# Accumulating block 1's first product pair by pair, with four accumulators in two PSUM banks

## The chip, the core and the metric

The kernel runs on one core of a Trainium2 chip. The metric is the device time of one execution in microseconds (us); of the kernel before, three timed runs gave 608.89, 608.99 and 609.29 us, median 608.99. Engines are called as the profile calls them: PE (TensorE), DVE (VectorE), ACT (ScalarE), POOL (GpSimd), and SP, whose queue issues all the loads spoken of here.

## The reference

A block-and-window attention over 2 batches, 8 heads, 768 positions and head size 64 is followed by two feed-forward layers on the 1536 resulting tokens of width 512:

```python
k_sum = k.reshape(B, H, nb, 32, D).max(axis=3)
v_sum = v.reshape(B, H, nb, 32, D).mean(axis=3)
scores = concat([where(abs(i - j) < 16, scale * q @ k.T, -1e9), scale * q @ k_sum.T + log(32)])
x = softmax(scores) @ concat([v, v_sum])          # tokens x 512
...
h = x @ w_in
x = (max(h, 0) + alpha * min(h, 0)) @ w_out       # 512 -> 2048 -> 512
...
h = x @ w_in
out = (h * sigmoid(h)) @ w_out                    # 512 -> 2048 -> 512
```

## The kernel before

Every fp32 product of the feed-forward layers is made of three fp32r matmuls on high and low pieces: `three` (lines 278 to 283) issues low weights by high input, high by low, and high by high into one PSUM tile. The attention works on blocks of `QB` = 256 tokens (six blocks) and on pairs of heads (four pairs), so it has 24 steps, numbered here 0 to 23 in the order of line 638: block 0 and block 1 alternate over the four pairs (steps 0 to 7), then blocks 2, 3, 4 and 5 follow with four steps each. A step runs through these stages:

- the scores `sc` on PE (L523), into the one PSUM tile that the pool `ps_s` has, so that the next step's scores wait until the last have been read;
- scale, mask and maximum, `t` (L531) and `nm` (L540), on DVE;
- the exponentials `e` with their sums `sm` on ACT (L548), the reciprocal `rs` on DVE (L557, L559), and the product of both on POOL (L560);
- the transposes `pt` on PE (L566), copied by ACT to `pT`; the values `o` on PE (L579), copied by ACT (`xh`, L587) and split by DVE (`xl`, L588).

Beside it run the preparations. `prep_k` makes block maxima of the keys on DVE (L465, L471); `prep_v1` sums the values on POOL (L482) and DVE (`vr`, L485). The weights are loaded by `load_next` (L116), turned from halves into high and low pieces by three DVE operations (L142, L146, L149), an ACT copy (L155) and a POOL subtraction (L156). The values of the second batch and the weights from the fourth tile on land in the same two buffers `raw` (pool `stage`, `STAGE` = 2), so a load waits until an earlier tile has been read.

The first feed-forward layer's first product of block 0 is made in `first_in` (line 719) one pair at a time, five steps behind the attention: four accumulators, each in a PSUM bank of its own, of which 256 of 512 columns are used. The pool `ps_mm` has six banks, and `pt`, `pv` and `o` rotate in what is left. Blocks 1 to 5 are made by `in_item` (line 296), which takes two of the four column tiles at once, all four pairs in a row, and so begins when the block's attention is done. `activate` makes both Relu halves on ACT (L324, L325), their sum on DVE (L328), a high piece on ACT (L336) and a low piece on POOL (L337); `out_pair` (line 345) makes the second product.

All this code is written out in the order of keys (`at`, line 644: a step's number plus the constants of lines 26 to 32). The tile framework then reorders it: it plays the instructions through on a timeline of its own and places each on its engine where it expects it to be ready. On the chip each engine keeps the order that results, so an instruction that waits holds all that is behind it on its engine.

The text counts *products*: the PE matmuls of L281 to L283, from the first on. Block 0's and block 1's first products are 48 each.

## Time and profile before

| | |
|---|---|
| median of three runs | 608.99 us (608.89 to 609.29) |
| span of the profiled execution, first to last instruction | 604.6 us |
| PE busy | 576.8 us, 95% of the span |
| DVE busy | 424.0 us, 70% |
| ACT busy | 277.5 us, 46% |
| POOL busy | 72.3 us, 12%, all of it in the first 160 us |

The profiled execution's time as a whole is not among the profile's figures; its span is 4.4 us under the median. Shares of the whole span hide the two parts of this kernel: PE is busy without a break after the first 64 us, while before that it has gaps and DVE has none. "Busy" counts the time from an instruction's start to its end, and a matmul's end is modelled: back to back, the next one starts well before the modelled end of the one before it.

### The profile page before, as it was taken

What the parts mean: (1) busy time and instruction counts of PE and PEld (TensorE: products, weight loads), DVE (VectorE), ACT (ScalarE), POOL (GpSimd) and SP (SyncE); (2) the same over time, 40 slices, a digit from 0 to 9 for tenths busy, and PEclk for the clock granted to TensorE, in tenths of its full rate; (3) what the DMA queues carried; (4) which work ended last, traced back from release to release, by engine and by line L of the source; (5) the groups of instructions that cost most, each with busy time, mean ns of one, the idle gap of its engine ahead of it and who ended that gap; (6) DMA issues with size and microseconds to landing.
All of it is one profiled execution on the core that took longest, in us unless ns stands there. A gap on an engine that the chain in (4) does not pass through costs nothing.

```text
span 604.6 us, 8927 instructions
## 1 busy us (share of the span) xinstructions
PE 576.8 (95%) x3428; PEld 483.5 (80%) x3428; DVE 424.0 (70%) x747; ACT 277.5 (46%) x636; POOL 72.3 (12%) x69
## 2 busy tenths in 40 slices
PE   2777999999999999999999999999999999999997
PEld 1556788999888888888888888888888888888886
DVE  3899979548995484349696879885972499965312
ACT  2768977654543341424544645543621245333200
POOL 2657654232100000000000000000000000000000
PEclk9988999999999999999999999999999999999999
DMA  9958754002351040003022002333130032200112
GB/s 263 341 193 260 231 147 140 2 2 70 140 154 56 0 140 0 1 1 112 28 69 70 1 1 79 131 117 93 32 108 0 1 111 96 73 1 0 54 69 88
DMA packets 31771, 52.54 MB, mean 87 GB/s; under 512 B 2288, under 2 KB 20976, under 8 KB 31728
## 3 DMA queue, kind: packets, MB, share of 16 engines
q1 hardware_dynamic: 31728, 51.97, 27.2%
q8 instruction: 27, 0.44, 0.3%
q14 instruction: 16, 0.13, 0.1%
HBM read 48.82 MB, written 3.15 MB: 86 GB/s over the span
## 4 chain that ended last, share of the span: by engine, by line
PE 82%; DVE 9%; DMA 3%; ACT 2%; SPq 1%; issue 1%; POOL 0%; DVEq 0%; POOLq 0%
PE ps L281 27%; PE ps L282 27%; PE ps L283 27%; DVE w L146 2%; DMA y<-in_w 1%; DVE w L149 1%; DMA vs<-in_vw 1%; DVE w L142 1%; DVE t L531 1%; DVE sm L557 1%; DVE nm L540 1%; PE o L579 1%; DVE kT L465 1%; ACT e L548 1%; DMA raw<-in_w 1%
## 5 line engine op out<-in xcount | busy, mean ns | idle before, releaser
L281 PE MATMUL ps<-xh,wl 128*128 128x512 f32 (+1 forms) x352 | 127.5, 367 | 1.2 <-ACT xh L587 1.2
L282 PE MATMUL ps<-xl,wh 128*128 128x512 f32 (+1 forms) x352 | 127.9, 364 | 0.0
L283 PE MATMUL ps<-xh,wh 128*128 128x512 f32 (+1 forms) x352 | 127.4, 363 | 0.0
L282 PE MATMUL ps<-gl,wh 128*128 128x512 f32 (+1 forms) x240 | 83.3, 348 | 0.0
L283 PE MATMUL ps<-gh,wh 128*128 128x512 f32 (+1 forms) x240 | 82.9, 346 | 0.0
L281 PE MATMUL ps<-gh,wl 128*128 128x512 f32 (+1 forms) x240 | 82.5, 350 | 0.0
L336 ACT CAST gh<-g 128x512 fp32r<-128x512 f32 x96 | 59.3, 622 | 46.2 <-PE ps L283 24.2
L281 PEld LDWEIGHTS ps<-xh,wl 128*128 128x128 f32 x352 | 66.5, 191 | 12.4 <-POOL e L560 1.4
L282 PEld LDWEIGHTS ps<-xl,wh 128*128 128x128 f32 x352 | 67.3, 191 | 10.2 <-issue 0.2
L283 PE MATMUL ps<-wh,gh 128*128 128x512 f32 (+1 forms) x196 | 75.4, 385 | 0.0
L283 PEld LDWEIGHTS ps<-xh,wh 128*128 128x128 f32 x352 | 67.3, 191 | 10.1
L282 PE MATMUL ps<-wl,gh 128*128 128x512 f32 (+1 forms) x196 | 75.4, 385 | 0.0
L281 PE MATMUL ps<-wh,gl 128*128 128x512 f32 (+1 forms) x196 | 75.2, 385 | 0.1
L337 DVE TENSOR_TENSOR gl<-g,gh 128x512 fp32r<-128x512 f32 x84 | 57.5, 687 | 20.7 <-ACT gh L336 20.3
L394 DVE TENSOR_TENSOR y<-ps,y 128x512 f32<-128x512 f32 x48 | 32.8, 689 | 45.4 <-PE ps L283 45.2
L324 ACT ACTIVATE g<-ps 128x512 f32<-128x512 f32 (+1 forms) x50 | 29.0, 579 | 70.8 <-PE ps L283 69.9
L155 ACT CAST wh<-w 128x512 fp32r<-128x512 f32 x64 | 39.3, 622 | 48.0 <-DVE w L149 43.5
L328 DVE SCALAR_TENSOR_TENSOR g<-m,nal,g 128x512 f32<-128x512 f32 (+1 forms) x60 | 41.4, 705 | 25.0 <-ACT m L325 24.9
L281 PEld LDWEIGHTS ps<-gh,wl 128*128 128x128 f32 x240 | 45.2, 189 | 6.6 <-issue 0.5
L282 PEld LDWEIGHTS ps<-gl,wh 128*128 128x128 f32 x240 | 45.4, 189 | 6.1 <-POOL gl L337 0.2
L283 PEld LDWEIGHTS ps<-gh,wh 128*128 128x128 f32 x240 | 45.3, 189 | 5.6
L146 DVE SCALAR_TENSOR_TENSOR w<-raw,w 128x512 uint32<-128x512 uint32 x61 | 44.6, 741 | 0.3
(82 smaller groups left out, 867.1 us busy)
## 6 DMA issues: line engine op xcount, KB each, us to landing
raw<-in_w SPq DMA_DIRECT2D x61, 512.0 KB, 3.8
vs<-in_vw SPq DMA_DIRECT2D x16, 288.0 KB, 5.6
kT<-in_kT SPq DMA_DIRECT2D x8, 480.0 KB, 5.2
q<-in_qT SPq DMA_DIRECT2D x24, 128.0 KB, 4.1
out<-y SPq DMA_DIRECT2D x11, 256.0 KB, 2.0
y<-in_vT SPq DMA_DIRECT2D x4, 384.0 KB, 6.5
y<-in_w SPq DMA_DIRECT2D x3, 512.0 KB, 7.7
raw<-in_vT SPq DMA_DIRECT2D x4, 384.0 KB, 4.5
```

The costliest lines, as they stand in the source:

```text
L142: nc.vector.tensor_scalar(out=w, in0=high, scalar1=3, scalar2=0x3FFFFFFF, op0=ALU.logical_shift_left, op1=ALU.bitwise_and,)
L146: nc.vector.scalar_tensor_tensor(out=w, in0=high, scalar=0xC0000000, in1=w, op0=ALU.bitwise_and, op1=ALU.bitwise_or)
L149: nc.vector.scalar_tensor_tensor(out=w, in0=low, scalar=29, in1=w, op0=ALU.logical_shift_right, op1=ALU.bitwise_or)
L155: nc.scalar.copy(out=hi, in_=w)
L281: nc.tensor.matmul(ps, all_, bh, start=first, stop=False)
L282: nc.tensor.matmul(ps, ah, bl, start=False, stop=False)
L283: nc.tensor.matmul(ps, ah, bh, start=False, stop=last)
L324: nc.scalar.activation(out=g[:, j * w:(j + 1) * w], in_=ps, func=AF.Relu)
L328: nc.vector.scalar_tensor_tensor(out=g[:, at], in0=m[:, at], scalar=nal[:, f + j:f + j + 1], in1=g[:, at], op0=ALU.mult, op1=ALU.add,)
L336: nc.scalar.copy(out=gh, in_=g)
L337: (nc.gpsimd if early else nc.vector).tensor_tensor(out=gl, in0=g, in1=gh, op=ALU.subtract)
L394: nc.vector.tensor_tensor(out=at, in0=src, in1=at, op=ALU.add)
```

## The change

`first_in` now takes the block as an argument and is called for blocks 0 and 1, each one pair at a time, again five steps behind. Block 1 is taken out of the list of `in_item`s, and the list that interleaves the two products is shifted, so that both items of a block's first product stand ahead of the second product of the block before. Two accumulators of 256 columns share one bank: the first one's first matmul clears the bank's flags, the second one's first matmul is issued without a clear, and a dependency without a semaphore keeps it behind the first. `activate` gets one bank of 512 columns in place of two of 256, so ACT reads it with two instructions in place of four. No matmul is added or taken away.

```diff
-    def three(ps, a, b, first, last):
+    def three(ps, a, b, first, last, again=False):
 
         (ah, all_), (bh, bl) = a, b
-        nc.tensor.matmul(ps, all_, bh, start=first, stop=False)
+        i = nc.tensor.matmul(ps, all_, bh, start=first, stop=False, skip_group_check=again)
...
+        return i
...
-    def in_k(u, i, k, ps):
+    def in_k(u, i, k, ps, first=None):
...
-            k == 0, k == KT - 1,
+            k == 0 if first is None else first, k == KT - 1, first is not None,
...
-        ins = [(i, in_item, units[i], f, 2) for i in range(1, NBLK) for f in range(0, CF, 2)]
+        ins = [(i, in_item, units[i], f, 2) for i in range(2, NBLK) for f in range(0, CF, 2)]
...
-            seq += ins[max(0, 2 * i - 1):2 * i + 1]
+            seq += ins[max(0, 2 * i - 2):2 * i] if i else []
...
-        def first_in(p):
-
-            if not acc:
-                acc.extend(ps_mm.tile([P, 512], F32, tag="mm", name="ps")[:, :QB] for _ in range(CF))
+        def first_in(blk, p):
+
+            if blk not in acc:
+                acc[blk] = [ps_mm.tile([P, 512], F32, tag="mm", name="ps") for _ in range(CF // 2)]
             need(p + 1)
-            for i in range(CF):
-                in_k(units[0], i, p, acc[i])
-                if p == NPAIR - 1 and i % 2:
-                    activate(units[0], i - 1, 2, acc[i - 1:i + 1])
+            for i in range(0, CF, 2):
+                ps = acc[blk][i // 2]
+                one = in_k(units[blk], i, p, ps[:, :QB], p == 0)
+                two = in_k(units[blk], i + 1, p, ps[:, QB:], False)
+                if p == 0:
+                    tc.add_manual_dep(
...
+                if p == NPAIR - 1:
+                    activate(units[blk], i, 2, [ps])
                     rests()
...
-            if blk == 0:
-                at(k + AT_IN, first_in, p)
+            if blk < 2:
+                at(k + AT_IN, first_in, blk, p)
```

The framework makes a new order of it on every engine. Two places are shown, as the built programs hold them (in the changed kernel lines after 283 are one higher).

The first is on DVE, around step 9's scores. Before, after `t` of step 9 come the last of the weight tile `w_305`, key maxima, and only much later the sum `vr` of the fifth tile of values, out of the buffer `raw_771`:

```order
L531 SCALAR_TENSOR_TENSOR t_642<-sc_633,cst_93 128x480
L146 SCALAR_TENSOR_TENSOR w_305<-raw_250,w_305 128x512
L465 TENSOR_REDUCE kT_599<-kT_599 128x24
L540 TENSOR_REDUCE nm_644<-t_642 128x4
L149 SCALAR_TENSOR_TENSOR w_305<-raw_250,w_305 128x512
L557 TENSOR_SCALAR sm_602<-sm_602 128x4
L588 TENSOR_TENSOR xl_79<-o_607,xh_78 128x256
L471 COPY kT_599<-kT_599 128x6x24
L531 SCALAR_TENSOR_TENSOR t_701<-sc_692,cst_93 128x480
L465 TENSOR_REDUCE kT_648<-kT_648 128x24
L559 RECIPROCAL rs_623<-sm_602 128x4
L485 TENSOR_REDUCE vr_965<-raw_771 128x24
```

After, that sum (here `vr_1020`, out of `raw_807`) stands ahead of step 9's `t`, and the next weight tile `w_1059` is begun ahead of step 10's `t`; it is loaded into the buffer that the sum has to free:

```order
L486 TENSOR_REDUCE vr_1020<-raw_807 128x24
L466 TENSOR_REDUCE kT_611<-kT_611 128x24
L532 SCALAR_TENSOR_TENSOR t_666<-sc_657,cst_93 128x480
L558 TENSOR_SCALAR sm_614<-sm_614 128x4
L472 COPY kT_611<-kT_611 128x6x24
L589 TENSOR_TENSOR xl_79<-o_619,xh_78 128x256
L541 TENSOR_REDUCE nm_668<-t_666 128x4
L560 RECIPROCAL rs_647<-sm_614 128x4
L142 TENSOR_SCALAR w_1059<-raw_1055 128x512
L532 SCALAR_TENSOR_TENSOR t_725<-sc_716,cst_93 128x480
```

So the sum has moved ahead of two steps' `t`, and the weight tile, which before began after step 12's `t`, ahead of step 10's.

The second place is where the scores of steps 17 to 20 stand. Before, DVE took step 17's `t` (`t_1331`) shortly after step 16's, ahead of the weight tile `w_1204`:

```order
L531 SCALAR_TENSOR_TENSOR t_1226<-sc_1217,cst_93 128x480
L485 TENSOR_REDUCE vr_1152<-raw_1063 128x24
L557 TENSOR_SCALAR sm_1130<-sm_1130 128x4
L540 TENSOR_REDUCE nm_1228<-t_1226 128x4
L559 RECIPROCAL rs_1162<-sm_1130 128x4
L588 TENSOR_TENSOR xl_79<-o_1044,xh_78 128x256
L531 SCALAR_TENSOR_TENSOR t_1331<-sc_1322,cst_93 128x480
L328 SCALAR_TENSOR_TENSOR g_873<-m_876,nal_77,g_873 128x256 x2
L142 TENSOR_SCALAR w_1204<-raw_1200 128x512
```

After, step 17's `t` (`t_1360`) stands behind four weight tiles, of which `w_2118` is the last, and behind the evacuation `y` of the second product's last tile of block 1:

```order
L142 TENSOR_SCALAR w_2118<-raw_1425 128x512
L589 TENSOR_TENSOR xl_79<-o_1293,xh_78 128x256
L146 SCALAR_TENSOR_TENSOR w_2118<-raw_1425,w_2118 128x512
L149 SCALAR_TENSOR_TENSOR w_2118<-raw_1425,w_2118 128x512
L359 COPY y_80<-ps_1325 128x2x256
L532 SCALAR_TENSOR_TENSOR t_1360<-sc_1351,cst_93 128x480
L329 SCALAR_TENSOR_TENSOR g_1219<-m_1222,nal_77,g_1219 128x256 x2
L589 TENSOR_TENSOR xl_79<-o_1382,xh_78 128x256
L142 TENSOR_SCALAR w_2154<-raw_1458 128x512
L541 TENSOR_REDUCE nm_1362<-t_1360 128x4
L532 SCALAR_TENSOR_TENSOR t_1419<-sc_1410,cst_93 128x480
```

On PE the scores of steps 18, 19 and 20 now stand close together, with nine products between the first two and one between the last two (`sc_1502` is step 19's, `sc_1578` step 20's, `ps_1460` block 3's first product; before, 38 products lie between steps 19 and 20):

```order
L281 MATMUL ps_1460<-xh_78,wl_159 128x256
L282 MATMUL ps_1460<-xl_79,wh_158 128x256
L283 MATMUL ps_1460<-xh_78,wh_158 128x256
L524 MATMUL sc_1502<-kT_855,q_1001 64x120 x8
L281 MATMUL ps_1460<-xh_78,wl_192 128x256
L524 MATMUL sc_1578<-kT_611,q_1065 64x120 x8
L282 MATMUL ps_1460<-xl_79,wh_191 128x256
L283 MATMUL ps_1460<-xh_78,wh_191 128x256
```

What moved: the score step whose reading on DVE was early now waits behind weight conversion, and three score steps follow each other with little other PE work between them.

## Rows read from the trace of the kernel before

**Rows 1.** Busy time by stretch: length, then PE, PEld, DVE, ACT, POOL, then clock, DMA.

```profile
36.00:64.00 28.00, 21.00 (x278) 16.92 (x279) 27.96 (x56) 22.82 (x83) 17.81 (x15) 0.88 0.70 212
64.00:102.00 38.00, 37.96 (x423) 33.66 (x422) 33.06 (x66) 30.96 (x94) 22.27 (x20) 1.00 0.60 174
```

**Rows 2.** Timeline of PE: start, length (us), line, tiles, count, idle time before.

```profile
77.86 0.65 PE L566 MATMUL pt<-cst,e 128*120 128x128 f32 x4
...
102.46 0.63 PE L523 MATMUL sc<-kT,q 64*64 64x120 f32 x14 [0.50 <-DVE t L531]
...
109.92 0.64 PE L523 MATMUL sc<-kT,q 64*64 64x120 f32 x16
```

**Rows 3.** Timeline of PE, two products in a row at full clock.

```profile
63.83 0.28 PE L283 MATMUL ps<-xh,wh 128*128 128x256 f32 x1
63.95 0.28 PE L281 MATMUL ps<-xh,wl 128*128 128x256 f32 x1
```

**Rows 4.** Timeline of DVE around steps 8 to 11.

```profile
45.74 0.91 DVE L149 SCALAR_TENSOR_TENSOR w<-raw,w 128x512 uint32<-128x512 uint32 x1
...
50.29 0.94 DVE L465 TENSOR_REDUCE kT<-kT 128x24 f32<-128x768 f32 x1
...
55.37 0.31 DVE L485 TENSOR_REDUCE vr<-raw 128x24 f32<-128x192 f32 x1
```

**Rows 5.** Timeline of SP's queue, two loads into the buffers `raw`.

```profile
46.67 0.33 SPq L450 DMA_DIRECT2D raw<-in_vT  x1
...
55.71 0.33 SPq L116 DMA_DIRECT2D raw<-in_w  x1
```

**Rows 6.** DMA issues from 46 to 47.2 us: count, size, us to landing.

```profile
raw<-in_vT SPq DMA_DIRECT2D x1, 384.0 KB, 4.2
```

**Rows 7.** Timeline of POOL, the sum of the fifth tile of values.

```profile
51.45 1.99 POOL L482 TENSOR_TENSOR raw<-raw 128x384 f32<-128x384 f32 x2
```

**Rows 8.** All loads into the buffers `raw` from 30 to 105 us.

```profile
DMA to landing us min/median/max: 3.3/3.8/5.6
```

**Rows 9.** Timeline of DVE in a stretch in which POOL stands idle.

```profile
98.57 0.68 DVE L358 COPY y<-ps 128x512 f32<-128x512 f32 x1
99.17 0.68 DVE L149 SCALAR_TENSOR_TENSOR w<-raw,w 128x512 uint32<-128x512 uint32 x1
99.77 0.42 DVE L142 TENSOR_SCALAR w<-raw 128x512 uint32<-128x512 uint32 x1
100.10 0.41 DVE L588 TENSOR_TENSOR xl<-o,xh 128x256 fp32r<-128x256 f32 x1
100.44 0.68 DVE L146 SCALAR_TENSOR_TENSOR w<-raw,w 128x512 uint32<-128x512 uint32 x1
101.15 0.69 DVE L149 SCALAR_TENSOR_TENSOR w<-raw,w 128x512 uint32<-128x512 uint32 x1
101.76 0.65 DVE L531 SCALAR_TENSOR_TENSOR t<-sc,cst 128x480 f32<-128x480 f32 x1
102.33 0.87 DVE L328 SCALAR_TENSOR_TENSOR g<-m,nal,g 128x256 f32<-128x256 f32 x2
103.11 0.64 DVE L540 TENSOR_REDUCE nm<-t 128x4 f32<-128x480 f32 x1
103.68 0.41 DVE L588 TENSOR_TENSOR xl<-o,xh 128x256 fp32r<-128x256 f32 x1
```

**Rows 10.** Timeline of DVE after step 16's scores.

```profile
74.47 0.63 DVE L531 SCALAR_TENSOR_TENSOR t<-sc,cst 128x480 f32<-128x480 f32 x1
75.02 0.34 DVE L485 TENSOR_REDUCE vr<-raw 128x24 f32<-128x192 f32 x1
...
79.78 0.43 DVE L142 TENSOR_SCALAR w<-raw 128x512 uint32<-128x512 uint32 x1
```

**Rows 11.** Timeline of all engines, one moment at which POOL and DVE both work.

```profile
34.22 1.01 POOL L560 TENSOR_TENSOR e<-e,rs 128x480 f32<-128x480 f32 x1 [0.85 <-DVE rs L559]
...
34.42 1.36 DVE L146 SCALAR_TENSOR_TENSOR w<-raw,w 128x512 uint32<-128x512 uint32 x1
```

More of the change, by code (lines that the diff above doesn't have):

```diff
@@ L276, in rests @@
             pending.pop(0)()
-    def three(ps, a, b, first, last):
+    def three(ps, a, b, first, last, again=False):
         (ah, all_), (bh, bl) = a, b
-        nc.tensor.matmul(ps, all_, bh, start=first, stop=False)
-        nc.tensor.matmul(ps, ah, bl, start=False, stop=False)
-        nc.tensor.matmul(ps, ah, bh, start=False, stop=last)
+        i = nc.tensor.matmul(ps, all_, bh, start=first, stop=False, skip_group_check=again)
+        nc.tensor.matmul(ps, ah, bl, start=False, stop=False, skip_group_check=again)
+        nc.tensor.matmul(ps, ah, bh, start=False, stop=last, skip_group_check=again)
+        return i
     g_t = {}
-    def in_k(u, i, k, ps):
+    def in_k(u, i, k, ps, first=None):
         l, ch, t0, n, _ = u
@@ L686, in tile_blocks_attention_mlps @@
         spread_t = {}
-        acc = []
+        acc = {}
         def means(b, p):
@@ L717, in need @@
                 conv_op(at_conv[0])
-        def first_in(p):
-            if not acc:
-                acc.extend(ps_mm.tile([P, 512], F32, tag="mm", name="ps")[:, :QB] for _ in range(CF))
+        def first_in(blk, p):
+            if blk not in acc:
+                acc[blk] = [ps_mm.tile([P, 512], F32, tag="mm", name="ps") for _ in range(CF // 2)]
             need(p + 1)
-            for i in range(CF):
-                in_k(units[0], i, p, acc[i])
-                if p == NPAIR - 1 and i % 2:
-                    activate(units[0], i - 1, 2, acc[i - 1:i + 1])
+            for i in range(0, CF, 2):
[4 more added lines that the diff above has]
+                    tc.add_manual_dep(
+                        two.ins if hasattr(two, "ins") else two,
+                        (one.ins if hasattr(one, "ins") else one).name,
+                        mybir.DependencyInfo(mybir.DependencyClass.NoSync, mybir.DependencyReason.DATA),
+                        reason="the bank is cleared by its first product",
+                    )
+                if p == NPAIR - 1:
+                    activate(units[blk], i, 2, [ps])
                     rests()
```

2 lines of the change are left out of this document (1 added, 1 removed).

## The prediction

> **What bounds the kernel now.** Read busy time by stretch first. From 64 us on PE never stops (37.96 of 38 us), so a microsecond by which PE gets ahead of its work before that point shortens the kernel by one, unless PE has to wait again later. From 36 to 64 us it is the other way round: DVE is busy 27.96 of 28 us and PE only 21.00 [rows 1]. PE's 7.0 idle us there are the room into which the change puts work; DVE, which sets when each step of the attention is done, has no room at all. Then read PE's timeline to see where the two meet again: the last time that PE waits for anything is 0.50 us at 102.46, for step 18's `t` on DVE [rows 2]. DVE is thus not far behind PE until 102 us, and an order that lets PE run ahead must let DVE run ahead too.
>
> One point serves to compare both kernels: the end of step 20's scores at 109.92 + 0.64 = 110.56 us [rows 2]. By the two orders exactly the same PE work stands ahead of it in both kernels once the later of step 18's transposes and step 20's scores is done (scores 0 to 20, transposes 0 to 18, values 0 to 16, 288 products). All that follows is the same work at full clock with no PE wait in the trace. So the new time is the old one plus the shift of this point. The median is 608.99 and the span 604.6; the 4.4 us around the span are taken as unchanged.
>
> **What the change moves.** Block 1's 48 products leave the stretch after step 13's scores and go between steps 6 and 15. One product costs 63.95 - 63.83 = 0.12 us at full clock [rows 3], so 48 x 0.12 = 5.8 us are moved, less than the 7.0 us of room. But PE's order ahead of step 16's scores shows 110 products in place of 84: only 26 net, 26 x 0.12 = 3.1 us, are gained there, since block 0's second product, which stood between, now stands behind. That is the most that PE can be ahead while DVE keeps its times. On ACT four reads of 256 columns become two of 512, counted as nothing, since ACT has 5.2 us of idle time in the stretch [rows 1]; the clear-free first matmul and the dependency without a semaphore stand on PE in order and cost nothing; the number of banks held for the accumulators is four as before, and that the last two are held some products longer is covered by the first two, which come free when block 0 ends.
>
> **What DVE pays.** Up to step 16's `t` DVE has the same instructions ahead of it in both orders, plus one `xl` (103.11 + 0.57 to 103.68 and 100.44 - 100.10 = 0.34 us [rows 9]). Two of them now come earlier than their data.
>
> First, the sum `vr` of the fifth tile of values. It stood at 55.37 us; in the new order it has the place, counted in DVE instructions, that the key maxima of 50.29 us have now [rows 4]. Its load may start when the weight tile before it in the buffer has been read, and that ended at 45.74 + 0.91 = 46.65 us, with the issue at 46.67 [rows 4, 5]; the new order reaches that point at about the same time or half a microsecond sooner. The load lands 4.2 us later [rows 6], POOL takes 1.99 us [rows 7]: 46.2 + 4.2 + 2.0 = 52.4. DVE gets there at 50.3 to 50.8, so it waits 1.6 to 2.1 us; I take 1.6. Second, the weight tile begun ahead of step 10's `t` is loaded into the buffer that this sum frees: 52.7 + 0.1 + 3.8 (median landing [rows 8]) = 56.6. Between the sum and the weight tile DVE has key maxima 0.9, `t` 0.57, `nm` 0.57, `xl` 0.34 and three small ones of 0.1 to 0.2, about 2.8 us, so it arrives at 55.5 and waits 1.1; with the wait of step 10's `t` behind it, PE, ACT and POOL can't go on with the attention. Together 2.7 us on an engine that had no idle time. Off go about 0.3 us for a wait that falls away and 0.3 us for DVE work that no longer runs against POOL. Step 16's `t` moves from 74.47 [rows 10] to 74.5 + 0.3 + 2.7 - 0.6 = 76.9, and step 16's scores, four short DVE instructions ahead of it, end at 76.4.
>
> PE has 110 products done then. Before, the 110th was done at 77.86 [rows 2], with step 17's scores (0.6) and one small transpose (0.2) done as well. So PE is ahead by 77.9 - 76.4 - 0.8 = 0.7 us at that point, not by 3.1.
>
> **What comes late next.** In the new order step 17's `t` stands behind four weight tiles on DVE, and a chain of buffers runs through them. 34 products take PE to 80.7; DVE evacuates the second product (0.6) and sums the last values (0.3) by 81.6; the next weight tile can be loaded only then. Before, that load was landed and begun at 79.78, 4.4 us after the end of the sum at 75.36 [rows 10]; by the median landing of 3.8 it is 85.5. The tile after that waits for the next sum (86.1 + 3.9 = 90.0), its three operations take 0.33 + 0.71 + 0.60 = 1.64 [rows 9], to 91.7, and free the buffer for the fourth one (95.6). The third tile, a `g` (0.78) and an evacuation (0.60), 3.0 us in all, fit in that gap. Then 0.33 + 0.34 + 0.71 + 0.60 + 0.60 bring step 17's `t` to 98.2, its end 98.7; `g`, `xl`, a weight operation and `nm` (0.78 + 0.34 + 0.33 + 0.57) bring step 18's `t` to 100.7 to 101.3; two weight operations, `nm` and a sum (0.71 + 0.60 + 0.57 + 0.1) bring step 19's to 103.3 to 103.9. PE can't cover this: between the scores of 18 and 19 it has nine products, between 19 and 20 one. Step 20's scores end at 104.5. Then 14 products (1.7), transposes and values (1.2), 24 products (2.9) and step 18's transposes (0.6): 110.9, against 110.56. So PE's lead of 0.7 is used up in waits for three successive `t`, and 0.3 us is lost.
>
> This goes by DVE prices from a stretch in which POOL is idle [rows 9]. Where both work a weight operation took 1.36 us [rows 11] in place of 0.7. In the new order POOL has six operations beside the weight tiles; most of what they cost falls into the waits for loads, and I add 0.4 us, between 0 and 1.5. The sum is +0.7 us: 608.99 + 0.7 = **609.7 us**.
>
> On this point the Trainium skill has a rule, in "SBUF — State Buffer", section "Who interferes with whom": DVE and POOL share one pair of ports, which one of them holds for a whole instruction, and a DVE instruction with two inputs in SBUF is hit, a `tensor_reduce` never. The weight operation of 1.36 us, which reads two tiles, agrees, and so do the key maxima, 0.94 us beside a working POOL. By the rule alone, with every POOL operation next to the weight tiles hitting one, the 0.4 would be six times 0.6, or 3.6 us, an estimate that ends at 609.3 + 3.6 = 612.9; that lies at the far end of the slower rival below, which holds it with a chance of 0.03.
>
> **The rivals.** *PE keeps its lead (faster).* DVE may have slack that the trace doesn't show: some of its busy time is work drawn out by POOL, which shrinks when DVE waits, and the four weight tiles may find their loads landed. If the two early waits cost 0.5 in place of 2.7, PE is ahead by 2.9 at step 16, and if the `t` of steps 17 to 19 follow as PE comes, it keeps that: 606.1. For it: 7.0 us of room and PE's 95% share. Against it: DVE 27.96 of 28 busy. It decides at step 18's `t`: begun before 99.2, the kernel is faster by more than 1.2 us. *The buffer chain is longer (slower).* The same chain with landings nearer to the 5.6 us that one load took [rows 8]: 1.2 us more at the first sum and 1.0 more at one of the later tiles, 609.7 + 2.2 = 611.9. For it: each link stands behind the one before, and POOL can add up to 1.1 more than I took. It decides from a step 18 `t` begun after 101.6. *The moved products are not hidden.* The new order puts 24 more products ahead of step 8's scores, 2.9 us at full clock, while PE's room up to there is under 3 us; if `t` of steps 7 and 8 waits for PE, DVE loses about a microsecond more: 610.7.
>
> **How the numbers follow.** What a measurement of this kernel can tell from no change is about 0.2%, 1.2 us. Chances: the forecast's case 0.42, between 608.5 and 610.9, of which 0.35 lie within 1.2 us, 0.01 under and 0.06 over it; PE keeps its lead 0.26; the longer chain 0.27; products not hidden 0.05, of which 0.02 still lie within. Faster 0.27, same 0.37, slower 0.36. The range leaves out the best tenth of the faster case and of the slower one: 606.3 to 612.0; the forecast's own range is 608.5 to 610.9.
>
> **What would show it.** In the trace after: PE's idle time from 36 to 64 us smaller than 7.0; a DVE wait of 1 to 2 us for POOL ahead of `vr` at about 52 us and one for a load ahead of L142 at about 56; step 16's `t` at 76 to 77; step 18's `t` at 100 to 102, and PE waits of about 2 us ahead of the scores of step 20. The prediction is wrong if DVE shows no such waits, or if PE stays without a gap from 76 to 110 us.

## The result and the profile after

The changed kernel takes 614.8 us (median of four runs, 613.84 to 616.85), against 608.94 for the kernel before beside it: a ratio of 1.0100, with a 95% interval of 1.0078 to 1.0122. It is 5.9 us slower; +0.7 us was forecast, and the range ended at 612.0.

The first lines of the page after, span and PE's busy time:

```profile
span 612.1 us, 8902 instructions
...
PE 579.6 (95%) x3428; PEld 485.3 (79%) x3428; DVE 424.1 (69%) x747; ACT 279.5 (46%) x632; POOL 73.1 (12%) x69
```

The profiled execution took 613.84 us, 1.7 over its span; in 18 further profiles of this study the difference was 1.7 to 1.9. The kernel before's profiled execution (span 604.6) thus lasted some 606.4 us, 2.6 under its median, while the profile after is 1.0 under its own. So the spans differ by 7.5 us, 1.6 more than the medians. These 7.5 us are 2.8 of PE busy time (576.8 to 579.6, the same 3428 matmuls) and 4.7 of PE idle time (27.8 to 32.5). The stretches say where; columns as in [rows 1], first the changed kernel:

```profile
36.00:64.00 28.00, 23.69 (x265) 19.64 (x258) 25.97 (x50) 20.02 (x68) 17.16 (x16) 0.84 0.70 209
64.00:102.00 38.00, 34.64 (x404) 29.86 (x402) 32.10 (x62) 30.94 (x95) 22.30 (x20) 1.00 0.54 156
102.00:130.00 28.00, 25.12 (x294) 21.94 (x298) 18.08 (x41) 17.98 (x62) 8.43 (x9) 0.88 0.17 59
```

and the kernel before from 102 us on:

```profile
102.00:130.00 28.00, 27.54 (x323) 24.83 (x324) 16.84 (x41) 19.45 (x69) 10.11 (x10) 1.00 0.10 32
```

Against [rows 1], PE's idle time from 36 to 64 us fell from 7.0 to 4.3 us: the products did go where they were meant to. But from 64 to 102 us it rose from 0.0 to 3.4, and from 102 to 130 us from 0.5 to 2.9, with the clock granted at 0.88 in place of 1.00. The remaining 1.6 us of idle time lie ahead of 36 us.

PE around the first loss (four products and step 8's scores), then the scores of steps 18, 19 and 20 and step 18's transposes:

```profile
40.63 0.41 PE L282 MATMUL ps<-xl,wh 128*128 128x256 f32 x1
40.84 0.41 PE L283 MATMUL ps<-xh,wh 128*128 128x256 f32 x1
...
45.10 0.28 PE L281 MATMUL ps<-xh,wl 128*128 128x256 f32 x1
45.22 0.28 PE L282 MATMUL ps<-xl,wh 128*128 128x256 f32 x1
...
47.43 0.64 PE L524 MATMUL sc<-kT,q 64*64 64x120 f32 x16
...
104.28 1.08 PE L524 MATMUL sc<-kT,q 64*64 64x120 f32 x16 [2.73 <-DVE t L532]
...
109.06 1.08 PE L524 MATMUL sc<-kT,q 64*64 64x120 f32 x16
...
110.92 0.64 PE L524 MATMUL sc<-kT,q 64*64 64x120 f32 x16 [0.47 <-DVE t L532]
...
117.39 0.60 PE L567 MATMUL pt<-cst,e 128*120 128x128 f32 x4
```

DVE: `t` of step 6, two operations of the eighth weight tile and step 8's `t`; the wait for a load; step 16's `t`; five operations of later weight tiles; `t` of steps 17, 18 and 19:

```profile
38.57 0.62 DVE L532 SCALAR_TENSOR_TENSOR t<-sc,cst 128x480 f32<-128x480 f32 x1
...
47.84 1.13 DVE L142 TENSOR_SCALAR w<-raw 128x512 uint32<-128x512 uint32 x1
49.00 1.66 DVE L146 SCALAR_TENSOR_TENSOR w<-raw,w 128x512 uint32<-128x512 uint32 x1
50.58 0.64 DVE L532 SCALAR_TENSOR_TENSOR t<-sc,cst 128x480 f32<-128x480 f32 x1
...
57.70 0.43 DVE L142 TENSOR_SCALAR w<-raw 128x512 uint32<-128x512 uint32 x1 [1.51 <-DMA raw<-in_w]
...
80.06 0.65 DVE L532 SCALAR_TENSOR_TENSOR t<-sc,cst 128x480 f32<-128x480 f32 x1
...
92.50 0.67 DVE L142 TENSOR_SCALAR w<-raw 128x512 uint32<-128x512 uint32 x1 [0.46 <-DMA raw<-in_w]
93.20 1.65 DVE L146 SCALAR_TENSOR_TENSOR w<-raw,w 128x512 uint32<-128x512 uint32 x1
...
96.63 1.78 DVE L146 SCALAR_TENSOR_TENSOR w<-raw,w 128x512 uint32<-128x512 uint32 x1
...
98.94 1.18 DVE L149 SCALAR_TENSOR_TENSOR w<-raw,w 128x512 uint32<-128x512 uint32 x1
...
101.42 1.64 DVE L149 SCALAR_TENSOR_TENSOR w<-raw,w 128x512 uint32<-128x512 uint32 x1
...
103.59 0.64 DVE L532 SCALAR_TENSOR_TENSOR t<-sc,cst 128x480 f32<-128x480 f32 x1
...
106.17 0.64 DVE L532 SCALAR_TENSOR_TENSOR t<-sc,cst 128x480 f32<-128x480 f32 x1
110.21 0.66 DVE L532 SCALAR_TENSOR_TENSOR t<-sc,cst 128x480 f32<-128x480 f32 x1 [1.27 <-PE sc L524]
```

and POOL beside five of these operations (47.84, 93.20, 96.63, 98.94 and 101.42):

```profile
47.70 0.99 POOL L561 TENSOR_TENSOR e<-e,rs 128x480 f32<-128x480 f32 x1 [1.41 <-DVE rs L560]
...
92.85 1.46 POOL L156 TENSOR_TENSOR wl<-w,wh 128x512 fp32r<-128x512 f32 x1
...
96.32 1.54 POOL L156 TENSOR_TENSOR wl<-w,wh 128x512 fp32r<-128x512 f32 x1 [2.02 <-ACT wh L155]
97.83 1.74 POOL L338 TENSOR_TENSOR gl<-g,gh 128x512 fp32r<-128x512 f32 x1
...
100.85 1.67 POOL L156 TENSOR_TENSOR wl<-w,wh 128x512 fp32r<-128x512 f32 x1 [1.28 <-ACT wh L155]
```

In the kernel before, `t` of steps 6 and 8 on DVE, then step 8's scores on PE:

```profile
37.85 0.62 DVE L531 SCALAR_TENSOR_TENSOR t<-sc,cst 128x480 f32<-128x480 f32 x1
...
45.17 0.65 DVE L531 SCALAR_TENSOR_TENSOR t<-sc,cst 128x480 f32<-128x480 f32 x1
```

```profile
43.68 0.64 PE L523 MATMUL sc<-kT,q 64*64 64x120 f32 x16 [1.45 <-DVE t L531]
```

Three things are to be seen. Step 8's `t` comes 12.0 us after step 6's (38.57 to 50.58), against 7.3 before (37.85 to 45.17). Of these 4.7 us, 3.0 lie ahead of step 8's scores: PE starts them 8.9 us after step 6's `t` (38.57 to 47.43), before 5.8 (37.85 to 43.68), and it is never idle between the two `t`, where before it was idle for 1.7 us. The other 1.7 lie between the start of the scores and their `t` (3.2 us for 1.5), where DVE has the two operations of the eighth weight tile. Step 16's `t` is at 80.06, 5.6 us later than in [rows 10], 4.9 of them since step 6. And PE waits 2.73 us for step 17's `t`, with its scores and products at half speed after that.

### The profile page after: what moved, and what is told of

It reads as the page before. It is cut to its first block, busy times and chain, and to the rows that moved or that the text cites. A ratio compares the mean times of both kernels' runs of the same rounds, so it can differ in the third digit from the quotient of the medians.

```text
span 612.1 us, 8902 instructions
## 1 busy us (share of the span) xinstructions
PE 579.6 (95%) x3428; PEld 485.3 (79%) x3428; DVE 424.1 (69%) x747; ACT 279.5 (46%) x632; POOL 73.1 (12%) x69
## 3 DMA queue, kind: packets, MB, share of 16 engines
q1 hardware_dynamic: 31728, 51.97, 27.2%
## 4 chain that ended last, share of the span: by engine, by line
PE 82%; DVE 7%; DMA 5%; SPq 2%; issue 1%; ACT 1%; POOL 0%; DVEq 0%
PE ps L281 27%; PE ps L282 27%; PE ps L283 27%; DMA raw<-in_w 2%; DVE w L146 2%; DMA y<-in_w 1%; DVE w L142 1%; DMA vs<-in_vw 1%; DMA kT<-in_kT 1%; PE o L580 1%; DVE w L149 1%; DVE t L532 1%; ACT e L549 1%; SPq L461 1%; PE sc L524 1%
## 5 line engine op out<-in xcount | busy, mean ns | idle before, releaser
L281 PE MATMUL ps<-xh,wl 128*128 128x512 f32 (+1 forms) x352 | 129.3, 370 | 1.6 <-ACT xh L588 1.6
L281 PEld LDWEIGHTS ps<-xh,wl 128*128 128x128 f32 x352 | 67.2, 192 | 13.7 <-ACT xh L588 1.8
L329 DVE SCALAR_TENSOR_TENSOR g<-m,nal,g 128x512 f32<-128x512 f32 (+1 forms) x60 | 39.0, 666 | 34.4 <-ACT m L326 34.2
L325 ACT ACTIVATE g<-ps 128x512 f32<-128x512 f32 x48 | 28.7, 597 | 74.2 <-PE ps L283 71.0
L549 ACT ACTIVATE e<-t,nm 128x120 f32<-128x120 f32 x96 | 36.8, 387 | 19.1 <-DVE nm L541 15.8
```

The lines of the kernel that those rows point to most:

```text
L281: i = nc.tensor.matmul(ps, all_, bh, start=first, stop=False, skip_group_check=again)
L325: nc.scalar.activation(out=g[:, j * w:(j + 1) * w], in_=ps, func=AF.Relu)
L329: nc.vector.scalar_tensor_tensor(out=g[:, at], in0=m[:, at], scalar=nal[:, f + j:f + j + 1], in1=g[:, at], op0=ALU.mult, op1=ALU.add,)
L549: nc.scalar.activation(out=e[:, u, :], in_=t[:, u, :], func=AF.Exp, bias=nm[:, u:u + 1], accum_out=sm[:, u:u + 1],)
```

## The experiments

All of them, with what the text uses (beside them, the kernel before's median lay between 608.5 and 609.4 us): the ratio to the kernel before (95% interval), the time from step 6's `t` to step 16's on DVE's timeline, PE's idle time from 64 to 130 us, and the time from 36 to 130 us at the lower clock (twice what the granted clock of each of the stretches 36 to 64, 64 to 90 and 90 to 130 us is short of 1, times its length; the levels are 1.2 and 2.4 GHz). The last two columns go by fixed times, while step 6's `t` lies between 37.0 and 41.1 us in these profiles, so they are rough.

| kernel | us | ratio | steps 6 to 16 | idle 64:130 | low clock |
|---|---|---|---|---|---|
| before | 608.9 | 1 | 36.6 | 0.5 | 6.7 |
| changed | 614.8 | 1.0078 to 1.0122 | 41.5 | 6.2 | 16.2 |
| e1 list as before | 612.2 | 1.0038 to 1.0075 | 41.2 | 5.3 | 10.1 |
| e2 list only | 613.0 | 1.0041 to 1.0078 | 40.0 | 3.9 | 11.6 |
| e3 banks only | 619.1 | 1.0139 to 1.0199 | 40.2 | 5.2 | 27.7 |
| e4 weights later | 614.8 | 1.0067 to 1.0126 | 39.7 | 6.6 | 17.3 |
| e5 block 1 one step later | 618.2 | 1.0117 to 1.0185 | 40.9 | 9.1 | 17.6 |
| e6 the same, list as before | 622.6 | 1.0191 to 1.0246 | 44.5 | 9.7 | 27.2 |
| e7 block 1 two steps later | 614.4 | 1.0067 to 1.0115 | 41.1 | 6.1 | 9.9 |
| e8 2.5 later, list as before | 623.3 | 1.0189 to 1.0248 | 41.1 | 12.8 | 20.3 |
| e9 DVE order early | 615.2 | 1.0052 to 1.0119 | 41.8 | 8.3 | 6.7 |
| e10 DVE order early, late | 612.1 | 1.0022 to 1.0071 | 42.7 | 4.1 | 13.7 |
| e11 before, less DVE work | 612.0 | 1.0002 to 1.0061 | 35.0 | 3.2 | 12.9 |
| e12 changed, less DVE work | 611.5 | 1.0000 to 1.0046 | 52.7 | 4.7 | 12.7 |
| e13 e1, fewer products | 613.2 | 1.0041 to 1.0084 | 42.1 | 4.3 | 23.9 |
| e14 before, fewer products | 614.6 | 1.0053 to 1.0110 | 34.9 | 6.6 | 23.3 |
| e15 two score tiles | 620.9 | 1.0157 to 1.0223 | 34.4 | 7.9 | 23.4 |
| e16 e10, list as before | 612.5 | 1.0024 to 1.0064 | 44.4 | 3.8 | 13.7 |
| e17 before, one key | 612.1 | 1.0039 to 1.0068 | 36.5 | 5.5 | 17.0 |
| e18 before, one key | 616.5 | 1.0108 to 1.0146 | 37.5 | 5.3 | 20.6 |

**One part undone, or one part alone.** The first theory put the loss where it was seen last, at the `t` of steps 17 to 20 behind weight conversion (late); its rival put it in the 5 us already lost by step 16 (early).

```diff
-            seq += ins[max(0, 2 * i - 2):2 * i] if i else []
+            seq += ins[max(0, 2 * i - 3):2 * i - 1] if i else []
```

> The changed kernel with one thing undone: the list of products alternates half by half again, as in the kernel before, while block 1's first product is still accumulated pair by pair in shared banks. By the two orders PE is the same as in the changed kernel up to product 174 and DVE up to step 16's t; then step 17's t stands behind 10 weight tiles on DVE in place of 13. Late theory (the time is lost where the t of steps 17 to 20 stand behind weight conversion and the second product): step 17's t begins within 3 us of step 16's scores as PE reaches it, near 82 us in place of 103.6; what is left of the loss is that of step 18, 609 to 611.5 us. Early theory (the 5 us by which step 16's scores are late are already lost there): step 16's t at 79 to 81 us again and 613.5 to 615 us.

612.2 us. Step 16's `t` follows step 6's by 41.2 us, as in the changed kernel, so the early loss is all there; step 17's `t` comes at 93.2 in place of 103.6, and PE gets its full clock from 64 us on. The late part is worth some 2.6 us (614.8 to 612.2). The rest isn't in the list.

The list alone, in the kernel before:

```diff
-            seq += ins[max(0, 2 * i - 1):2 * i + 1]
+            seq += ins[2 * i:2 * i + 2]
```

> The kernel before with the shifted list alone: block 1's first product is made all four pairs in a row by in_item as before, in banks of its own, but both halves of a block's first product stand ahead of the second product of the block before. By the orders DVE is as before up to step 14's t; step 17's t then stands behind 13 weight tiles and 2 evacuations, as in the changed kernel (13 and 4). Late theory: 612.5 to 615 us, with PE waits of 2 to 3 us for t between 95 and 110 us. Early theory (pair-by-pair accumulation in 36 to 64 us is the cause): 608.5 to 610 us. If shared banks are the cause: 608.5 to 610 us.

613.0 us: the list alone costs 3.6 us by its ratio, by a jump at step 15's `t` (8 us after step 14's) and PE waits of 3.9 us between 64 and 130. The shares of the list and of the rest don't simply add.

Shared banks for block 0 alone (`in_k` and `three` as in the changed kernel):

```diff
-                acc.extend(ps_mm.tile([P, 512], F32, tag="mm", name="ps")[:, :QB] for _ in range(CF))
+                acc[blk] = [ps_mm.tile([P, 512], F32, tag="mm", name="ps") for _ in range(CF // 2)]
```

> The kernel before with shared banks alone: block 0's four accumulators stand in two banks, one clear for each bank, ACT reads 512 columns at a time; block 1 and the list are as before. This frees two banks for the transposes and values, and the order that results has the scores of steps 13 to 19 earlier among the products. Theory that sharing itself costs nothing: 607.5 to 610 us, and the products into the shared banks 0.12 us apart at full clock as others are. Theory that sharing costs (products into a bank half cleared, or 512-column reads that hold PE): 611 us or more, and such products more than 0.12 us apart or PE waits for ACT at L281 of 1 us and more.

619.1 us, more than the whole change costs. PE's timeline of this run, three products into shared banks:

```profile
49.74 0.28 PE L283 MATMUL ps<-xh,wh 128*128 128x256 f32 x1
49.86 0.28 PE L281 MATMUL ps<-xh,wl 128*128 128x256 f32 x1
49.98 0.28 PE L282 MATMUL ps<-xl,wh 128*128 128x256 f32 x1
```

They start 0.12 us apart, as in [rows 3]: a product into a shared bank has its usual price. The time went into 5.2 us of PE waits after 64 us and 27.7 us at the lower clock, in place of 6.7.

```diff
-CONV2, CONV2_STEP = 14.0, 1.5
+CONV2, CONV2_STEP = 18.0, 1.5
```

> The changed kernel with CONV2 at 18 in place of 14: the ninth to twelfth weight tiles are asked for later. By the orders DVE is the same as in the changed kernel up to step 9's t; the weight tile ahead of step 10's t, for whose load DVE waited 1.51 us, is gone from there, step 17's t stands behind 8 weight tiles in place of 13, step 18's behind 12. Late theory: step 16's t 1.5 to 3 us earlier than the changed kernel's 80.1, step 17's t near 80 in place of 103.6 us, 610 to 612.5 us. Early theory: the 1.5 us of the one wait are all that is gained, 613 to 613.5 us.

614.8 us: nothing gained, though step 16's `t` now follows step 6's by 39.7 us in place of 41.5. Step 17's `t` comes at 81.0, as the late theory wanted, and the wait ahead of step 10's is gone; step 18's is at 104.6 instead.

**Block 1's products later.** The next theory had two places: an extra weight tile ahead of step 8's `t`, and the tiles ahead of step 17's. Calling block 1's `first_in` later takes both away, by DVE's order.

```diff
-                at(k + AT_IN, first_in, blk, p)
+                at(k + AT_IN + 1.0 * blk, first_in, blk, p)
```

> The changed kernel with block 1's products called six steps behind the attention in place of five; list and banks as in the changed kernel. By the orders step 7's t stands behind 6 weight tiles on DVE (7 in the changed kernel), step 8's behind 7 (8), step 17's behind 9 (13), step 18's behind 9 (14); 14 of the 24 extra products still stand ahead of step 8's scores and all by step 9's. Two-place theory (4 to 5 us are lost between the t of steps 6 and 8, where a weight tile more stands ahead on DVE and runs against POOL; 2 to 3 us behind the weight tiles ahead of step 17): step 6 to step 8 takes 7 to 9 us (7.3 in the kernel before, 12.0 in the changed one), step 17's t follows step 16's within 5 us, and the time is 606.5 to 610 us. Rival (it is the moved products on PE that hold steps 7 to 9, whatever DVE's order): step 6 to step 10 as long as in the changed kernel (19.4 us, 16.0 before, less than 1 us saved) and 612 to 614 us.

> As the run with block 1's products one step later, and the list of products alternating half by half as in the kernel before. DVE's order is the same up to step 18's t; then step 19's t stands behind 11 weight tiles and 2 evacuations in place of 13 and 4, step 20's behind 13 in place of 14. Two-place theory: nothing is left to gain early, and late only what the t of steps 19 and 20 still cost: 606 to 609.5 us, at most 1.5 us under that run. Rival (moved products): as that run, 611.5 to 614 us.

(e6: with the list edit of e1 as well.)

> The changed kernel with block 1's products called seven steps behind the attention: 24 products stand ahead of step 8's scores as in the kernel before and 42 ahead of step 10's (36 before, 62 in the changed kernel), DVE's order is the kernel before's up to about step 10. But step 17's t stands behind 12 weight tiles and 2 evacuations, nearly as in the changed kernel (13 and 4). Two-place theory: steps 6 to 8 take 7 to 8.5 us, so 3 to 4.5 us of the loss are gone; the late part stays, with step 17's t 10 us and more behind step 16's: 610 to 612 us. If the late part alone were the cause: 613.5 to 615 us. If the early part alone were: 608 to 609.5 us.

> Block 1's products called seven and a half steps behind the attention, and the list half by half as before. DVE's order is the kernel before's up to about step 10; step 17's t stands behind 10 weight tiles and 2 evacuations, step 18's behind 11, step 19's behind 12, step 20's behind 14: the weight tiles are spread over the steps in place of standing ahead of one. Two-place theory: 606 to 609 us. If spreading the tiles doesn't help (DVE is simply too late for PE from 76 to 110 us): 610 to 612 us.

(2.0 and 2.5 in place of 1.0, the last with the list edit too.) Measured: 618.2, 622.6, 614.4 and 623.3 us. Steps 6 to 8 did shrink as that theory wanted, from 12.0 to 9.5, 9.6, 8.5 and 8.5 us. But steps 8 to 16 then took 31.4 to 34.9 us (29.5 in the changed kernel), three of four runs are worse than the changed kernel, and the two-place theory falls: few weight tiles ahead of a `t` are no protection. What e8 shows from 90 to 102 us, then PE's waits for `t` from 36 us on (total, times, longest), and two of them in PE's timeline:

```profile
90.00:102.00 12.00, 3.16 (x36) 2.41 (x37) 11.11 (x18) 5.30 (x11) 6.28 (x5) 0.53 0.47 144
```

```profile
PE sc L524 <- DVE t L532: 15.1, 7, 4.0
```

```profile
93.40 1.08 PE L524 MATMUL sc<-kT,q 64*64 64x120 f32 x16 [3.60 <-DVE t L532]
...
98.50 1.08 PE L524 MATMUL sc<-kT,q 64*64 64x120 f32 x16 [4.01 <-DVE t L532]
```

In that order the scores of steps 18, 19 and 20 follow step 17's with no product between them (all four stand behind 168), while DVE has a weight tile between one `t` and the next. PE is idle for 8.8 of 12 us, with other products queued behind these scores. So it isn't DVE's order alone that counts but DVE's and PE's together: how much PE has between two score steps against what DVE has between their two `t`.

**DVE's order fixed by hand.** Dependencies without a semaphore keep the first operation of chosen weight tiles behind a step's `t`:

```diff
+BEHIND = {6: 7, 7: 8, 8: 12}
...
-        nc.vector.tensor_scalar(
+        behind(BEHIND.get(at_conv[0] - 1), nc.vector.tensor_scalar(
```

> The changed kernel with three orders fixed on DVE: the seventh weight tile's first operation stands behind step 7's t, the eighth's behind step 8's, the ninth's behind step 12's, each by a dependency without a semaphore. With that the weight tiles and value sums ahead of each t up to step 16 are those of the kernel before (6 and 4 at step 7, 7 and 4 at step 8, 8 and 4 at step 10, 9 and 6 at step 13), while PE keeps the changed order (48 products ahead of step 8's scores, 60 ahead of step 9's, 110 ahead of step 16's). Step 17's t still stands behind 12 weight tiles. If DVE's order is what loses the early part: step 6 to step 8 takes 7 to 8.5 us (7.3 before, 12.0 in the changed kernel), step 16's t follows step 6's by 36 to 38.5 us (36.6 before, 41.5 changed), 610.5 to 612.5 us. If PE's moved products lose it (scores behind products, at half clock): step 6 to 16 takes 40.5 us or more, 613.5 us or more.

615.2 us, as the theory of the moved products had it. `t` of steps 6, 8 and 16:

```profile
40.81 0.63 DVE L545 SCALAR_TENSOR_TENSOR t<-sc,cst 128x480 f32<-128x480 f32 x1
...
51.52 0.65 DVE L545 SCALAR_TENSOR_TENSOR t<-sc,cst 128x480 f32<-128x480 f32 x1
...
82.57 0.65 DVE L545 SCALAR_TENSOR_TENSOR t<-sc,cst 128x480 f32<-128x480 f32 x1
```

10.7 us from step 6 to step 8 (12.0 in the changed kernel) and 41.8 to step 16: with the tiles where they stood before, 1.3 us are gained between steps 6 and 8, and by step 16 nothing is. The place of the weight tiles is thus not the main cause of the early loss.

With four more tiles fixed behind the `t` of steps 17 to 20 (`9: 17, 10: 18, 11: 19, 12: 20`):

> As the run with the early DVE order fixed, and the tenth to thirteenth weight tiles fixed one each behind the t of steps 17, 18, 19 and 20. On PE 88 products stand between the scores of steps 16 and 17, 42 between 17 and 18, 9 and 11 between the next two. If a score step loses when DVE has more work between two t than PE has products between the scores: step 17's t comes as soon as PE gets there (88 to 92 us in place of 103.6), PE waits of about 2 us each stay ahead of the scores of steps 19 and 20 (one weight tile of 1.8 us and the step's own 2 us against 9 and 11 products, 1.1 and 1.3 us): 609.5 to 612 us. If only the number of tiles ahead of step 17 counts: no PE wait for t after 76 us and 607 to 609 us.

612.1 us, 3.1 less than e9. Step 17's `t` in this run:

```profile
96.64 0.66 DVE L545 SCALAR_TENSOR_TENSOR t<-sc,cst 128x480 f32<-128x480 f32 x1 [4.40 <-PE sc L537]
```

DVE now waits for PE there, and PE waits only 0.15 us for a `t` after 76 us. This is the late loss, found a second time at about the size of e1 (the intervals of e9's and e10's ratios overlap). The waits of 2 us ahead of steps 19 and 20 that were expected didn't come. With e1's list on top:

> The run with the order of weight tiles fixed early and late, with the list half by half as before. On PE 64 products stand between the scores of steps 16 and 17, 8 between 17 and 18, 58 between 18 and 19, 9 to 16 between 19 and 20. If both late remedies work on the same loss, they don't add: 611 to 612.5 us, as either alone. If they add: 608.5 to 610 us, and what is left is the early loss.

612.5 us: the two remedies work on the same loss.

**Work taken away.** If DVE had no time left to let PE be ahead, less DVE work must bring the moved products' gain out:

```diff
-        nc.vector.scalar_tensor_tensor(
-            out=w, in0=high, scalar=0xC0000000, in1=w, op0=ALU.bitwise_and, op1=ALU.bitwise_or
-        )
+        if not CF <= at_conv[0] - 1 < 14:
+            nc.vector.scalar_tensor_tensor(
+                out=w, in0=high, scalar=0xC0000000, in1=w, op0=ALU.bitwise_and, op1=ALU.bitwise_or
+            )
```

(and the same for the third operation, L149.)

> The kernel before with the second and third DVE operation of the fifth to fourteenth weight tile left out (20 operations of 0.7 to 1.4 us, so those tiles' weights are wrong; PE, ACT, POOL and the loads do the same work). It is the base for the same cut in the changed kernel. If DVE sets the attention's pace from 36 to 64 us: PE's 7.0 idle us there shrink to 2 to 4 us and the time is 603 to 606.5 us. If PE or ACT set it: 607.5 to 609.5 us.

> The changed kernel with the same 20 DVE operations left out. If the moved products bring nothing only because DVE has no time left for PE to be ahead of: this kernel is 1 to 4 us faster than the kernel before with the same cut. If the order on PE itself loses the time (scores of several steps close together, products moved ahead of scores): it stays 3 to 6 us slower than that kernel.

612.0 and 611.5 us, neither theory's numbers. The two are alike, so with a lighter DVE the change costs nothing and brings nothing; but the kernel before itself became no faster without 16 us of DVE work (424.0 to 408.0 busy). Nine of the operations left out, 9.3 us in the kernel before, stood between the `t` of steps 6 and 16; this stretch shrank by 1.6 us only, and DVE was idle for 5.2 us of it in place of 0.6. DVE, 27.96 of 28 us busy in [rows 1], did not set the pace alone. The framework made a new order for e11 and e12 too, so what a lighter DVE is worth by itself isn't shown. In e12 step 16's scores stand behind 192 products (84 before, 110 in the changed kernel), hence the 52.7 us in the table: that column is the pace of the attention and not the time lost.

Then PE's work: of block 1's first product only one matmul in three, in e1's kernel and in the kernel before:

```diff
+        if one_of_three[0]:
+            i = nc.tensor.matmul(ps, ah, bh, start=first, stop=last, skip_group_check=again)
+            return i
```

> The changed kernel with the list half by half (as the first run), and of block 1's 48 pair-by-pair products only the 16 of high by high pieces: the others are left out, so that product is inexact. 76 products stand ahead of step 16's scores in place of 110, at the same places. If the early loss is the PE time of the moved products, which stand ahead of scores: step 16's t comes 36 to 38 us after step 6's (41.2 in the first run), and the time is at most 1 us over that of the kernel before with the same cut, 604.5 to 606.5 us. If it is something else in the changed order: 40 us and more, and 607.5 to 609 us, which is the first run's 612.2 less 32 products of 0.12 us.

> The kernel before with the same cut: of block 1's 48 products only the 16 of high by high pieces, all four pairs in a row as before. The base for the run above. PE is busy without a gap from 64 us, so 32 products of 0.12 us less make it 3.8 us faster: 604.5 to 606 us. If it is less than 2 us faster, PE isn't what bounds the kernel before after 64 us.

613.2 and 614.6 us. e13 still needs 42.1 us from step 6 to 16, so the PE time of the moved products isn't all of the early loss. But between steps 6 and 8 it is the larger part. e13's `t` of these steps, then step 8's scores:

```profile
38.77 0.62 DVE L536 SCALAR_TENSOR_TENSOR t<-sc,cst 128x480 f32<-128x480 f32 x1
...
48.09 0.65 DVE L536 SCALAR_TENSOR_TENSOR t<-sc,cst 128x480 f32<-128x480 f32 x1
```

```profile
45.08 0.64 PE L528 MATMUL sc<-kT,q 64*64 64x120 f32 x16 [0.43 <-DVE t L536]
```

Steps 6 to 8 take 9.3 us here in place of 12.0: PE starts step 8's scores 6.3 us after step 6's `t` (8.9 in the changed kernel, 5.8 before), while the 3.0 us from there to step 8's `t` stay (3.2 and 1.5). In all runs with one score tile the first of these times follows the number of products ahead of step 8's scores: 4.9 to 5.8 us with 24 products (before, e2, e3, e7, e8, e11, e14, e17, e18), 6.3 with 32 (e13), 6.2 and 7.0 with 38 (e6, e5), 8.2 to 9.4 with 47 or 48 (changed, e1, e4, e9, e10, e12, e16). The second is 1.7 us in e10 and e16 and 2.5 in e9, where the weight tiles are fixed. So of the 4.7 us the 3.0 ahead of the scores go with the moved products, and the 1.7 behind them, wholly or in part, with the place of the weight tiles. What e13 gained by step 8 it lost by step 16 (32.8 us from step 8 on, 29.5 in the changed kernel), in an order of its own.

And the kernel before is 4.9 us slower by its ratio (1.0081) for 3.8 us less of PE work. Its stretch from 64 to 102 us, and the two largest PE waits in it:

```profile
64.00:102.00 38.00, 31.38 (x355) 26.38 (x354) 30.36 (x65) 29.83 (x99) 21.00 (x19) 0.86 0.62 173
```

```profile
80.50 1.08 PE L572 MATMUL pt<-cst,e 128*120 128x128 f32 x4 [3.52 <-DVE xl L594]
...
99.65 0.70 PE L585 MATMUL o<-pT,vs 120*64 120x64 f32 x8 [2.47 <-issue]
```

PE idles 6.6 us where the kernel before idles 0.04. The framework had made another order for the smaller work, and that order cost more than the work saved.

**A second score tile** (e3's kernel with `bufs=2` in `ps_s` and four banks in `ps_mm` during the attention):

```diff
-        ps_s = scope0.enter_context(tc.tile_pool(name="ps_s", bufs=1, space=bass.MemoryType.PSUM))
+        ps_s = scope0.enter_context(tc.tile_pool(name="ps_s", bufs=2, space=bass.MemoryType.PSUM))
```

> The kernel before with shared banks for block 0 (as the run with banks only), and the two banks that this frees spent on a second score tile: the attention has two score tiles and four other banks, and after it six other banks again. If the loop through the single score tile (scores, t, next scores) sets the pace up to step 16: step 16's t comes 32 to 35 us after step 6's (36.6 before) and the time is 604 to 608 us. If the pace is set elsewhere: 36 us and more, and since the scores of steps 13 to 19 stand earlier among the products than before, 611 to 619 us as in the run with banks only.

Steps 6 to 16 take 34.4 us, the shortest of all, as the theory of the single score tile wanted; the time is 620.9 us all the same. A faster attention up to step 16 is worth nothing if PE then waits 7.9 us after 64.

**The order alone.** The last two runs leave all work as it is and change one number of a key.

```diff
-AT_LATER, ITEM_STEP = 3.5, 0.8
+AT_LATER, ITEM_STEP = 3.5, 0.9
```

> The kernel before with ITEM_STEP at 0.9 in place of 0.8; the work is the same, instruction for instruction. Both orders are the kernel before's up to step 15; then step 17's scores stand behind 84 products (110 before), step 18's behind 168 to 174 (182 to 240), step 19's behind 175, step 20's behind 264, step 18's t behind 12 weight tiles and 2 evacuations on DVE (14 and 4). If the loss belongs to the changed work (moved products, shared banks): 608 to 610 us. If it belongs to where the score steps fall among weight tiles and products: step 16's t 36 to 37 us after step 6's as before, and PE waits for t of 2 us and more between 76 and 112 us: 611 to 618 us.

```diff
-AT_IN = 5.3
+AT_IN = 5.8
```

> The kernel before with AT_IN at 5.8 in place of 5.3; the work is the same. Both orders are the kernel before's up to step 15; then step 18's scores stand behind 144 to 174 products (182 to 240 before), step 19's behind 180 (249), step 20's behind 271 (288), and step 18's t behind 12 weight tiles. If the loss belongs to the changed work: 608 to 610 us. If it belongs to where the score steps fall: 611 to 616 us, with PE waits for t between 76 and 112 us.

612.1 and 616.5 us, 1.0053 and 1.0127. Up to step 16 both keep the pace of the kernel before (36.5 and 37.5 us). From 64 to 102 us, e17 (the profile is of the slowest of its eight executions, 615.56 us) and its largest PE wait there, then e18 and its:

```profile
64.00:102.00 38.00, 32.51 (x386) 27.94 (x385) 26.51 (x60) 28.64 (x93) 18.72 (x19) 0.93 0.60 159
```

```profile
81.48 0.39 PE L281 MATMUL ps<-xh,wl 128*128 128x256 f32 x1 [1.77 <-DVE xl L588]
```

```profile
64.00:102.00 38.00, 32.69 (x388) 27.61 (x387) 30.07 (x62) 30.38 (x98) 21.05 (x19) 0.94 0.60 171
```

```profile
99.04 0.39 PE L491 MATMUL pv<-cst,vr 128*24 128x128 f32 x1 [3.36 <-DVE xl L588]
```

No product was moved across the attention and no bank shared, and 3 to 8 us are gone, each time at other instructions: a product behind `xl`, a transpose behind `xl`. The places differ from the expected waits for `t`; that the loss is the order's is as expected.

No kernel of the study beats the one before.

## Why the prediction was wrong

**What held.** The comparison point: step 18's transposes end at 117.39 + 0.60 = 117.99, 7.4 us after the 110.56 of before, and the spans differ by 7.5. The direction of the moves: 2.7 us of PE's idle time from 36 to 64 us were filled (3.1 at most were given). The load wait ahead of L142 was 1.51 us for the 1.1 taken; the chain of loads ran at 88.3 and 92.5 where 85.5 and 90.0 were worked out, so it started 3 us late and had about the forecast's spacing (4.2 us for 4.5).

**The step that failed first** is "What DVE pays": 2.7 us on an engine said to set the pace, by counting the instructions ahead of step 16's `t`. Step 16's `t` came at 80.06 for 76.9, 3.2 us beyond the sum (0.7 of them stood already at step 6). 4.7 us were lost between steps 6 and 8, which are no term of the sum: PE, never idle there, came to step 8's scores 3.0 us later, behind the moved products, and DVE to their `t` another 1.7 us later, behind a weight tile that ran against POOL. The sum passed over this tile, because it is made up for by step 16; but steps 8 to 16 took 29.5 us for 29.3 with four weight operations on DVE in place of seven, and DVE was idle for 3.5 us of them in place of 0.6. The wait for POOL ahead of `vr` (1.6) did not occur: POOL was done at 52.51, near the 52.4 worked out, but DVE was late and came there at 53.10. The assumption under it, that DVE alone sets the pace, was wrong: 9.3 us less of DVE work made steps 6 to 16 of the kernel before 1.6 us shorter (e11), and the old places of the weight tiles didn't give the old pace back (e9). An engine busy for 27.96 of 28 us looked like the bound; these runs suggest that much of its work only filled the waits of a loop through PE, ACT and POOL.

**The rival with the chance of 0.05**, products not hidden, named the right steps (7 and 8) and the mechanism of the larger part; its price of 1 us was too small: 3.0, with DVE's part 4.7. It reckoned 24 more products at 0.12 us against a room of under 3 us. Between step 6's `t` and step 8's scores PE made 34 products in place of 8, the first of them at the lower clock, where they start 0.21 us apart (40.63 to 40.84), and its idle time up to those scores had been 1.5 us. That e13, with a third of those products, needs as long up to step 16 shows that this is not the whole of it. What couples steps 6 to 16 in the orders with shared banks (39.7 us and more, but for the run with two score tiles) stays open.

**Late**, the order of events was the forecast's and its sizes were not. From step 16's `t` to step 17's took 23.5 us for 21.3: four weight operations met a POOL subtraction and took 1.65, 1.78, 1.18 and 1.64 us in place of 0.7, which is some 3.5 us more, where 0.4 had been added for POOL altogether. The trace agrees here with the Trainium skill's rule ("SBUF — State Buffer", section "Who interferes with whom"), that the engine which comes second waits for the whole of the other's instruction: all four DVE operations end 0.55 us after the POOL operations that began 0.3 to 1.1 us ahead of them. After PE's wait of 2.73 us the scores took 1.08 us in place of 0.64; the clock after a wait was no term of the sum. From step 18's `t` to step 19's another 1.4 us went (4.0 us for 2.6): step 19's `t` waited 1.27 us for its scores, which stand on PE behind nine products at the lower clock. 3.2 + 2.2 + 1.4 = 6.8 of the 7.1 us by which step 20's scores (111.56) missed the 104.5 of the forecast; PE's lead over DVE was gone from step 17 on, as the text had it.

**The base** was wrong with little harm to the sum: of the 4.4 us around the span only 1.8 lie there; the profiled execution was 2.6 us quicker than the median.

**What was missing as a case.** The forecast weighed the moved work, and let the new order keep the old one's quality elsewhere. e17, e18 and e14 show that an order of the same or less work, made anew by the framework, loses 3 to 8 us here. The kernel before's order, without a PE gap from 64 to 102 us, was the exception among all that were run. Of the 5.9 us, some 3 are shown to hang on the list and the weight tiles ahead of steps 17 to 20 (e1, e10). Where the attention loses its early 4.7 us is shown as well, but not that they are the rest of the 5.9: in all runs of the changed kernel that shortened steps 6 to 8 by a microsecond and more or fixed its weight tiles (e5 to e10, e13, e16), steps 8 to 16 took 31 to 35 us in place of 29.5, and none got rid of the whole loss.

## What to carry to other kernels

Where a framework re-sorts a tightly interleaved kernel, an edit's price is first the price of a new order: change one key that should not matter in the kernel before, and see by how much that moves the time, ahead of any sum over moved instructions. Idle time of one engine inside a loop through four engines is room only if nothing in that loop stands behind what is put there, and an engine that is 99.9% busy need not be the bound: take some of its work away to see. Compare, step by step, what two engines have queued between the same two steps; scores that follow each other closely on PE while DVE has a weight tile between their `t` cost PE the difference, and then its clock.

## What the runs showed of the hardware

The start differs between executions: step 6's `t` lay between 37.0 and 41.1 us in the profiles of all these kernels, and in e17, which has the order of the kernel before up to step 15, it came 2.3 us later than there (PE had waited 4.98 us for loads of `q`, at a place where it waited 3.32 before) while the next ten steps took the same 36.5 us. Times of two profiles are to be compared from a step on, not from the span's start.

In that same run the clock was granted at 0.79 from 36 to 64 us, against 0.88 before, at the same pace: the lower clock cost nothing there, where PE still stood idle for 6.6 of 28 us, waiting for other engines.

An L142, which reads one tile, took 1.13 us at 47.84 beside the POOL operation of 47.70, for 0.42 elsewhere, and ended 0.28 us after it; the sum had taken only operations with two inputs to be held up. The same section of the Trainium skill says that a `tensor_scalar` can enter a mode that uses the shared ports too.
